# Sparse attention and a two-layer network: the second half of each value tile with its block sums in the first rows, and each half loaded by its own transfer

## The chip, the core and the metric

The kernel runs on one core of one Trainium2 chip. The metric is the device time of one execution in microseconds (us), and a kernel's time is the median over its runs. Each core has five engines with a queue of instructions of its own: TensorE (PE, matmuls; PEld are its weight loads), VectorE (DVE), ScalarE (ACT), GpSimd (POOL) and SyncE (SP). In this kernel SP issues every transfer between the chip's memory (HBM) and the core's working memory (SBUF); matmuls write into a second, smaller memory, PSUM. Engines wait for each other, and for transfers, through semaphores.

## The reference, cut to what matters

There are 4 batches, 8 heads, 768 positions and 64 numbers per head. A query sees the keys less than 16 positions away, and besides them 24 summaries, one for each block of 32 positions. Its key is the block's maximum, its value the block's mean, and its score gets log(32) added. One softmax runs over both, and the result goes through two dense layers with a squared ReLU between them.

```python
k_sum = k.reshape(B, H, nb, block, D).max(axis=3)
v_sum = v.reshape(B, H, nb, block, D).mean(axis=3)
scores_l = scale * np.matmul(q, k.transpose(0, 1, 3, 2))
mask_l = np.abs(pos[:, None] - pos[None, :]) < window
scores_s = scale * np.einsum('bhsd,bhnd->bhsn', q, k_sum) + np.log(block)
a = softmax(concatenate([where(mask_l, scores_l, -1e9), scores_s], axis=-1))
x = np.matmul(a, concatenate([v, v_sum], axis=2))   # then (3072, 512)
h = np.maximum(x @ w_in, 0.0)
out = h * h @ w_out                                  # d_ff = 2048
```

## The kernel before, in words

The 3072 rows are cut into 24 tiles of 128 queries (`g`, six to a batch), and each tile into two halves of 64 queries (`s` = 0 and 1). A half needs 96 keys, its own 64 and 16 on either side, and the 24 block sums of its batch: 120 columns of scores, and 120 rows of values. In the score columns and in the value tile `v_sb`, both halves have the keys in places 0 to 95 and the sums in places 96 to 119.

For each tile and head the kernel does this. `scores` multiplies queries and keys into the `s_ps` banks of PSUM. `mask_max` (DVE) adds the mask and finds the row maximum, `exponentials` (ACT) takes the exponential with the row sum, `inverse` and `norm` (DVE, then POOL) divide by that sum, and `turn` (DVE, 32x32 blocks) or `turn_pe` (PE) transposes the weights into `pT`. `outputs` multiplies them with `v_sb`: 8 matmuls, one a head, for half 0, and then 8 for half 1. `high_x` (ACT) and `low_x` (DVE) split the result into the two parts in which the dense layers take it. `ffn1` and `ffn2` are those layers, for two tiles (256 rows, a chunk) at a time. A float32 matmul shows as two records in the trace, one of the dense layers as one.

The values come by `load_v`, one transfer of 384 KB for both halves of a tile, into rows 0 to 95 of one of two buffers, `v_sb[g % 2]`. A buffer is free again when `outputs` of the tile two before it is done. The value sums are put into rows 96 to 127 of both halves by `place_v0` (batch 0: DVE copies out of PSUM, tokens VC) or `place_v` (later batches: DVE and POOL). The key sums go into chunk 4 of `k_sb` by `place_k` (tokens PK). For the first four tiles `scores_kt` takes keys straight from the transposed keys in `padded` and sums from `ksums`, with two matmuls for each head and half, one for 96 keys and one for 24 sums.

The order of the work on each engine is the order in which the program is written. The start, up to the end of the first two chunks, is a list of tokens (`START`): `L:v1` loads values of tile 1, `S2.0=01` scores of tile 2, `O3=2` the outputs of tile 3, `VC0v` a copy of value sums on DVE (v), ACT (a) or POOL (p), `F1.2.0` and `F2.2.0` steps of the two layers, and `Z6` six matmuls with zeros that fill time. Around the change its order on PE is the scores of tile 4, O1, O0, turning of tiles 2 and 3, the first F1 step, O3, O2, and then the layers almost without a break. On SP it is q4, k4, v1, v0, three weight loads, v3, v2, more weights. After the start, `period` gives each 48 us stretch the same pattern: 8 slots of the dense layers for one chunk, and in their gaps the attention of the next two tiles.

Transfers have eight semaphores (DMAHW0 to 7), taken in turn. So a transfer is not issued before the one eight places ahead of it in SP's queue has landed, and SP holds everything behind it meanwhile.

Of the kernel before, what the change touches and what calls it, by code (L numbers as in the profile page):

```python
# [11 lines left out]
F32 = mybir.dt.float32  # L12
# [58 lines left out]
def attn_ffn_kernel(ctx: ExitStack, tc: tile.TileContext, q, k, kt, v, vt, v0, w, consts, out):  # L73
    nc = tc.nc
    scale = 1.0 / math.sqrt(D)

    const = ctx.enter_context(tc.tile_pool(name="const", bufs=1))
# [9 lines left out]
    mask_sb = consts_sb[:, 0 : 3 * NK].rearrange("q (m c) -> q m c", m=3)  # L87
    id_sb, mean_sb = consts_sb[:, 3 * NK : 3 * NK + P], consts_sb[:, 3 * NK + P :]

    k_sb = [const.tile([P, 5, 2, NPAIR, NB], F32, name=f"k_sb{i}") for i in range(2)]  # L90

    v_sb = [const.tile([P, 2, DM], F32, name=f"v_sb{i}") for i in range(2)]

    q_sb = [const.tile([P, 2, NPAIR, 64], F32, name=f"q_sb{i}") for i in range(2)]
# [3 lines left out]
    ksums = [const.tile([P, NPAIR, NB], F32, name=f"ksum{i}") for i in range(2)]  # L98
# [18 lines left out]
    nc.vector.memset(vsum, 0.0)  # L117
    for t_ in e_bufs + pT:
        nc.gpsimd.memset(t_, 0.0)

    def e_sb(g):
        return e_bufs[g % 2 if g < FROM_PAIRS else 0]

    def copy(eng, out, in_):
        nc.scalar.copy(out=out, in_=in_) if eng is nc.scalar else eng.tensor_copy(out=out, in_=in_)
# [3 lines left out]
        nc.sync.dma_start(out=q_sb[g % 2], in_=q[g // NT, g % NT])  # L129

    def load_k(g):
        nc.sync.dma_start(out=k_sb[g % 2][:, 0:4], in_=k[g - FROM_KT])

    def load_qk(g):
        load_q(g)
        load_k(g)

    def load_v(g):
        nc.sync.dma_start(out=v_sb[g % 2][0:96], in_=v[g // NT, g % NT].rearrange("s j c -> j s c"))

    def sum_v0(vn):

# [10 lines left out]

    def place_v0(ps, j, eng):
        for g in range(2):
            copy(
                eng, v_sb[g][96:128, :, j * P : (j + 1) * P],
                ps[j * 32 : j * 32 + 32, 0:P].unsqueeze(1).to_broadcast([32, 2, P]),
            )

    kv, padded = {}, {}

# [24 lines left out]
        nc.vector.tensor_scalar_mul(vsum[:, p, 0:NB], vsum[:, p, 0:NB], 1.0 / BLOCK)  # L187

    def place_k(g, eng=nc.vector):
        copy(eng, k_sb[g % 2][:, 4], ksums[g // NT % 2].unsqueeze(1).to_broadcast([P, 2, NPAIR, NB]))  # L190

    def place_v(g):
        dst = v_sb[g % 2][96:128]
        if g % 2 == 0:
            for a in range(4):
                nc.vector.transpose(
                    out=dst[:, 0, :].rearrange("a (p c) -> a p c", c=128)[:, :, a * 32 : a * 32 + 32],
                    in_=vsum[a * 32 : a * 32 + 32],
                )
        else:  # L200
            nc.gpsimd.tensor_copy(out=dst[:, 0, :], in_=v_sb[0][96:128, 0, :])
        nc.gpsimd.tensor_copy(out=dst[:, 1, :], in_=v_sb[0][96:128, 0, :])

    w_raw = {}

# [51 lines left out]
    s_ps, nmx, sm = {}, {}, {}  # L257

    def scores(g, p0, p1, banks=None):


        if g not in s_ps:
            at = banks or (g % 2 * 2, g % 2 * 2 + 1)
            s_ps[g] = [bank[n].rearrange("a (p k) -> a p k", p=NPAIR) for n in at]
        for p in range(p0, p1):
            for r, s in ((0, 0), (1, 1), (0, 1), (1, 0)):
                rs, ss = slice(r * 64, r * 64 + 64), slice(s * 64, s * 64 + 64)
                nc.tensor.matmul(  # L268
                    s_ps[g][r][ss, p, 0:NK], lhsT=q_sb[g % 2][rs, s, p, :], rhs=k_sb[g % 2][rs, :, s, p, :],
                    start=True, stop=True,  # L270
                )

    def scores_kt(g, p0, p1, banks=None):

        if g not in s_ps:
            at = banks or (g % 2 * 2, g % 2 * 2 + 1)
            s_ps[g] = [bank[n].rearrange("a (p k) -> a p k", p=NPAIR) for n in at]
        for p in range(p0, p1):
            for k0, k1 in ((0, 96), (96, NK)):
                for r, s in ((0, 0), (1, 1), (0, 1), (1, 0)):  # L280
                    rs, ss = slice(r * 64, r * 64 + 64), slice(s * 64, s * 64 + 64)
                    o = g * P + s * 64
                    keys = ksums[0][rs, p, :] if k0 else padded[p // 2][rs, p % 2, o : o + 96]
                    nc.tensor.matmul(  # L284
                        s_ps[g][r][ss, p, k0:k1], lhsT=q_sb[g % 2][rs, s, p, :], rhs=keys, start=True, stop=True
                    )

    def mask_max(g, h):
# [43 lines left out]

    def turn(g, n0, n1):

        blocks = [(i, j) for i in range(4) for j in ((0, 1, 3) if i % 2 == 0 else (1, 2, 3))]
        for i, j in blocks[n0:n1]:
            nc.vector.transpose(  # L337
                out=pT[g % 2][j * 32 : j * 32 + 32, :, i * 32 : i * 32 + 32],
                in_=e_sb(g)[i * 32 : i * 32 + 32, :, j * 32 : j * 32 + 32],
            )  # L340
# [325 lines left out]
def _masks():  # L666
    m = np.full((3, P, NK), MASKED * math.sqrt(D), np.float32)
    for i, t in enumerate((0, 1, NT - 1)):
        for r in range(P):
            s, u = divmod(r, 64)  # L670
            qp = t * P + s * 64 + u
            for j in range(96):
                kp = t * P - WINDOW + s * 64 + j
                if 0 <= kp < S and abs(qp - kp) < WINDOW:
                    m[i, r, j] = 0.0
        m[i, :, 96:] = np.log(BLOCK) * math.sqrt(D)
    return m


# [7 lines left out]
def _layouts(q, k, v):  # L687
    qd = q.reshape(B, NPAIR, 2, NT, 2, 64, D).transpose(0, 3, 2, 6, 4, 1, 5)
    kp = np.zeros((B, H, S + 2 * WINDOW, D), k.dtype)
    kp[:, :, WINDOW : WINDOW + S] = k  # L690
    vp = np.zeros((B, H, S + 2 * WINDOW, D), v.dtype)
    vp[:, :, WINDOW : WINDOW + S] = v
    kd = np.zeros((B, NT, 2, D, 4, 2, NPAIR, NB), k.dtype)
    vd = np.zeros((B, NT, 2, 96, H, D), v.dtype)
    for s in range(2):
        for t in range(NT):
            o = t * P + s * 64
            kd[:, t, :, :, :, s] = kp[:, :, o : o + 96].reshape(B, NPAIR, 2, 4, NB, D).transpose(0, 2, 5, 3, 1, 4)
            vd[:, t, s] = vp[:, :, o : o + 96].transpose(0, 2, 1, 3)
    return {  # L700
        "q": np.ascontiguousarray(qd).reshape(B, NT, P, 2, NPAIR, 64),
        "k": kd.reshape(B * NT, P, 4, 2, NPAIR, NB)[FROM_KT:],
        "kt": np.ascontiguousarray(k.transpose(0, 1, 3, 2)).reshape(B, NPAIR, P, S),
        "v": vd.reshape(B, NT, 2, 96, DM),
        "vt": np.ascontiguousarray(v.transpose(0, 1, 3, 2)).reshape(B, NPAIR, P, S),
        "v0": np.ascontiguousarray(v[0].reshape(H, NT, P, D).transpose(2, 1, 0, 3)).reshape(P, NT, DM),
    }
# [22 lines left out]
```

## Time and profile before

| | us |
|---|---|
| median of 3 runs | 610.71 (609.70 to 612.49) |
| the profiled execution, its own time | 609.38 |
| its span, first to last instruction | 607.6 |
| PE busy in the span | 595.7 |
| DVE, ACT, POOL busy | 385.6, 265.6, 105.0 |

The profiled execution's time is 1.78 us longer than its span: that is what lies around the program. A row of a timeline begins with the start and the length of a stretch of like instructions, both in us from the span's start; behind it in brackets stands how long the engine had been idle and what ended that. SPq is SP issuing transfers. "DMA to landing" counts from the start of an issue until the data are there, given as least, median and greatest. The granted TensorE clock was 1.00 throughout.

### The profile page before, as it was taken

Reading aid. Unit: us, or ns where it says so; the run is one execution under the profiler, and the core shown is the slowest. Engines: PE = TensorE matmul, PEld = TensorE weight load, DVE = VectorE, ACT = ScalarE, POOL = GpSimd, SP = SyncE. Lnnn points to the kernel's source line nnn. Section 1 sums busy time; section 2 is a strip of 40 time slices with the busy share of each in tenths; the row PEclk is TensorE's granted clock in tenths of the full one; section 3 lists DMA queues with packets and bytes.
Section 4 is the critical chain, followed back from the end, with each engine's and each line's share of the span. In section 5 each row is a group of like instructions: output and inputs, shape, how many; then the busy total and the mean of one; then the engine's idle time right before and its main releaser. Section 6 shows DMA issues by size and latency. Waiting matters only on the chain.

```text
span 607.6 us, 12942 instructions
## 1 busy us (share of the span) xinstructions
PE 595.7 (98%) x5232; PEld 536.8 (88%) x5232; DVE 385.6 (63%) x1063; ACT 265.6 (44%) x687; POOL 105.0 (17%) x97
## 2 busy tenths in 40 slices
PE   8799999999999999999999999999999999999997
PEld 6688899889899989999999989999989989998996
DVE  5889899777647837837545855865663763663121
ACT  4888874343253333433425325425424424422222
POOL 3745765311000101102101101102101010110000
PEclk9999999999999999999999999999999999999999
DMA  8999571350007006006006204202201400200000
GB/s 284 326 352 419 200 260 59 107 185 16 1 22 257 2 2 224 2 2 224 2 2 196 81 2 135 92 1 84 91 2 41 135 1 2 87 1 1 36 0 36
DMA packets 22187, 60.35 MB, mean 99 GB/s; under 512 B 2288, under 2 KB 2288, under 8 KB 20592
## 3 DMA queue, kind: packets, MB, share of 16 engines
q1 hardware_dynamic: 22128, 59.53, 28.6%
q8 instruction: 41, 0.67, 0.4%
q14 instruction: 18, 0.15, 0.1%
HBM read 53.23 MB, written 6.29 MB: 98 GB/s over the span
## 4 chain that ended last, share of the span: by engine, by line
PE 94%; DMA 4%; SPq 0%; ACT 0%; DVE 0%; issue 0%; POOL 0%; POOLq 0%
PE o_ps L425 44%; PE ph L381 39%; PE s_ps L381 4%; PE ph L351 3%; DMA v_sb<-in_v 3%; PE s_ps L268 3%; DMA kv<-in_kt 1%; PE s_ps L284 0%; ACT e_sb L304 0%; SPq L171 0%; PE s_ps L351 0%; POOL e_sb L324 0%; SPq L129 0%; DVE ksum L179 0%; DVE xl L368 0%
## 5 line engine op out<-in xcount | busy, mean ns | idle before, releaser
L381 PE MATMUL ph<-xh,w_sb 128*128 128x256 f32 x1376 | 241.9, 279 | 0.5 <-DVE xl L368 0.5
L425 PE MATMUL o_ps<-w_sb,gh 128*128 128x512 f32 x768 | 238.2, 392 | 0.0
L381 PEld LDWEIGHTS ph<-xh,w_sb 128*128 128x128 f32 x1376 | 213.4, 188 | 8.6 <-issue 1.3
L381 PE MATMUL ph<-xl,w_sb 128*128 128x256 f32 x688 | 190.8, 277 | 0.0
L425 PEld LDWEIGHTS o_ps<-w_sb,gh 128*128 128x128 f32 x768 | 137.2, 188 | 25.0 <-issue 0.3
L425 PE MATMUL o_ps<-w_sb,gl 128*128 128x512 f32 x384 | 151.3, 394 | 0.0
L400 DVE TENSOR_TENSOR ph<-ph,r 128x512 f32<-128x512 f32 x85 | 59.3, 698 | 143.1 <-ACT r L389 142.3
L389 ACT ACTIVATE r<-ph 128x512 f32<-128x512 f32 x84 | 49.9, 594 | 191.0 <-PE ph L381 190.9
L381 PEld LDWEIGHTS ph<-xl,w_sb 128*128 128x128 f32 x688 | 129.5, 188 | 0.0
L337 DVE STREAM_TRANSPOSE pT<-e_sb 32x256 f32<-32x256 f32 x240 | 104.6, 436 | 4.1 <-POOL e_sb L324 0.7
L304 ACT ACTIVATE e_sb<-e_sb,nmx 128x120 f32<-128x120 f32 x192 | 73.6, 385 | 74.3 <-DVE nmx L296 74.3
L324 POOL TENSOR_TENSOR e_sb<-e_sb,total 128x480 f32<-128x480 f32 x47 | 46.2, 991 | 321.7 <-DVE total L318 150.9
L425 PEld LDWEIGHTS o_ps<-w_sb,gl 128*128 128x128 f32 x384 | 72.3, 188 | 14.6
L395 ACT ACTIVATE gh<-r 128x512 fp32r<-128x512 f32 x94 | 59.4, 632 | 13.3 <-PE o_ps L425 6.6
L403 DVE TENSOR_TENSOR gl<-ph,gh 128x512 fp32r<-128x512 f32 x85 | 58.8, 691 | 9.3 <-DVE ph L400 0.5
L296 DVE CUSTOM_DVE_ANT_0 e_sb<-s_ps,consts_sb 128x120 f32<-128x120 f32 x180 | 40.7, 277 | 1.6 <-PE s_ps L284 0.9
L244 POOL TENSOR_TENSOR w_raw<-w_raw 128x1024 int32<-128x1024 int32 (+1 forms) x20 | 35.8, 1792 | 26.0 <-ACT w_raw L235 9.5
L304 ACT ACTIVATION_READ_ACCUMULATOR e_sb<-e_sb,nmx 128x1 f32 x192 | 36.1, 188 | 0.0
L368 DVE TENSOR_TENSOR xl<-ph,xh 128x512 fp32r<-128x512 f32 x22 | 15.2, 690 | 24.4 <-ACT xh L365 24.4
L381 PE MATMUL s_ps<-xh,w_sb 128*128 128x256 f32 x160 | 29.0, 282 | 0.0
L365 ACT CAST xh<-ph 128x512 fp32r<-128x512 f32 x22 | 12.9, 586 | 33.6 <-PE ph L351 33.6
L351 PEld LDWEIGHTS ph<-pT,v_sb 128*64 128x64 f32 x704 | 21.6, 138 | 5.2 <-issue 3.4
(79 smaller groups left out, 412.6 us busy)
## 6 DMA issues: line engine op xcount, KB each, us to landing
w_raw<-in_w SPq DMA_DIRECT2D x12, 1024.0 KB, 13.7
v_sb<-in_v SPq DMA_DIRECT2D x24, 384.0 KB, 4.9
k_sb<-in_k SPq DMA_DIRECT2D x20, 384.0 KB, 6.4
q_sb<-in_q SPq DMA_DIRECT2D x24, 256.0 KB, 5.9
kv<-in_kt SPq DMA_DIRECT2D x16, 384.0 KB, 5.7
out<-ob SPq DMA_DIRECT2D x24, 256.0 KB, 2.0
kv<-in_vt SPq DMA_DIRECT2D x12, 384.0 KB, 6.6
w_raw<-in_w SPq DMA_DIRECT2D x8, 512.0 KB, 7.7
```

Of the source, the lines that this page charges most:

```text
L244: nc.gpsimd.tensor_tensor(out=lo, in0=hi, in1=lo, op=ALU.add)
L296: nc.vector.tensor_tensor_reduce(out=e_sb(g)[:, h, 0:NK], in0=s_ps[g][h % 2][:, h // 2, 0:NK], in1=m, scale=-scale, scalar=3.0e38, op0=ALU ...
L304: nc.scalar.activation(e, e, AF.Exp, bias=nmx[g, half][:, i : i + 1], scale=-1.0, accum_out=sm[g, half][:, i, 0:1])
L324: eng.tensor_mul(out=e, in0=e, in1=sm.pop((g, half)).unsqueeze(2).to_broadcast([P, 4, NK]))
L337: nc.vector.transpose(out=pT[g % 2][j * 32 : j * 32 + 32, :, i * 32 : i * 32 + 32], in_=e_sb(g)[i * 32 : i * 32 + 32, :, j * 32 : j * 32 + ...
L351: nc.tensor.matmul(xp[o : o + 64, h // 2, s * 64 : s * 64 + 64], lhsT=v_sb[g % 2][:, s, h * 64 : h * 64 + 64], rhs=pT[g % 2][:, h, s * 64 ...
L381: nc.tensor.matmul(ph, lhsT=w_sb[f][:, w, cc * P : (cc + 1) * P], rhs=x[c][:, cc, :], start=(n == 0), stop=(n == 3 * NC4 - 1))
L389: nc.scalar.activation(r, ph, AF.Relu)
L395: nc.scalar.activation(gh, r, AF.Square)
L400: nc.vector.tensor_mul(out=ph, in0=ph, in1=r)
L403: nc.vector.tensor_sub(out=gl, in0=ph, in1=gh.bitcast(F32))
L425: nc.tensor.matmul(o_ps[c][tt], lhsT=g_[:, ts_], rhs=w_sb[f][:, w, DM:], start=(first and n == 0), stop=(last and n == 2),)
```

## The change

In the second half (`s` = 1) of every tile the 24 sums now have places 0 to 23, and the 96 keys places 24 to 119, turned by 8: key j stands at place 24 + (j + 8) mod 96. The first half stays as it was. Keys, values and masks are laid out to fit on the host. In the kernel:

- `load_v` issues two transfers of 192 KB, half 0 into rows 0 to 95 and half 1 into rows 24 to 119.
- `place_v0` makes two copies of 128 columns (32 rows for half 0, 24 rows for half 1) in place of one of 2x128; `place_v` writes 24 rows for half 1.
- `k_sb` has ten chunks in place of 5x2: 0 the sums of half 1, 1 to 8 the keys of both, 9 the sums of half 0. `place_k` writes chunks 0 and 9, and `scores` takes every other chunk.
- `scores_kt` needs a third matmul for half 1, since its turned keys are two pieces (88 and 8 columns).
- `turn` transposes other blocks for half 1, as many as before: 12 a tile.
- Two memsets on POOL clear rows 96 to 127 of half 1 at the start, ahead of the memsets of `padded`.

```diff
+TURN = 8
+KEYS_AT = (
+    ((slice(0, 96), 0), (slice(96, NK), None)),
+    ((slice(NB + TURN, NK), 0), (slice(0, NB), None), (slice(NB, NB + TURN), 96 - TURN)),
+)
...
-    k_sb = [const.tile([P, 5, 2, NPAIR, NB], F32, name=f"k_sb{i}") for i in range(2)]
+    k_sb = [const.tile([P, 10, NPAIR, NB], F32, name=f"k_sb{i}") for i in range(2)]
...
+    for t_ in v_sb:
+        nc.gpsimd.memset(t_[96:128, 1], 0.0)
...
     def load_v(g):
-        nc.sync.dma_start(out=v_sb[g % 2][0:96], in_=v[g // NT, g % NT].rearrange("s j c -> j s c"))
+        for s, o in ((0, 0), (1, NB)):
+            nc.sync.dma_start(out=v_sb[g % 2][o : o + 96, s], in_=v[g // NT, g % NT, s])
...
         for g in range(2):
-            copy(
-                eng, v_sb[g][96:128, :, j * P : (j + 1) * P],
-                ps[j * 32 : j * 32 + 32, 0:P].unsqueeze(1).to_broadcast([32, 2, P]),
-            )
+            copy(eng, v_sb[g][96:128, 0, j * P : (j + 1) * P], ps[j * 32 : j * 32 + 32, 0:P])
+            copy(eng, v_sb[g][0:NB, 1, j * P : (j + 1) * P], ps[j * 32 : j * 32 + NB, 0:P])
...
-        copy(eng, k_sb[g % 2][:, 4], ksums[g // NT % 2].unsqueeze(1).to_broadcast([P, 2, NPAIR, NB]))
+        copy(eng, k_sb[g % 2][:, 0:10:9], ksums[g // NT % 2].unsqueeze(1).to_broadcast([P, 2, NPAIR, NB]))
...
-        nc.gpsimd.tensor_copy(out=dst[:, 1, :], in_=v_sb[0][96:128, 0, :])
+        nc.gpsimd.tensor_copy(out=v_sb[g % 2][0:NB, 1, :], in_=v_sb[0][96 : 96 + NB, 0, :])
...
-            for k0, k1 in ((0, 96), (96, NK)):
+            for n in range(3):
                 for r, s in ((0, 0), (1, 1), (0, 1), (1, 0)):
...
+                    if n == 2 and s == 0:
+                        continue
+                    to, first = KEYS_AT[s][n]
...
-        blocks = [(i, j) for i in range(4) for j in ((0, 1, 3) if i % 2 == 0 else (1, 2, 3))]
+        blocks = [(i, j) for i in range(4) for j in ((0, 1, 3), (1, 2, 3), (0, 1, 2), (0, 2, 3))[i]]
```

The order of the instructions shows the change at two places. The first is PE at O3 and O2, the outputs of tiles 3 and 2 in the start; pT_80 and v_sb_74 are the buffers of odd tiles, pT_79 and v_sb_73 those of even ones. Before:

```order
L351 MATMUL s_ps<-pT_80,v_sb_74 64x64 [waits DMAHW5_49,DVE_49]
L351 MATMUL s_ps<-pT_80,v_sb_74 64x64 x3
L351 MATMUL s_ps<-pT_80,v_sb_74 64x64 [waits Activation_49]
L351 MATMUL s_ps<-pT_80,v_sb_74 64x64 x11
L351 MATMUL ph<-pT_79,v_sb_73 64x64 [waits DMAHW6_49]
L351 MATMUL ph<-pT_79,v_sb_73 64x64 x3
L351 MATMUL ph<-pT_79,v_sb_73 64x64 [waits Activation_49]
L351 MATMUL ph<-pT_79,v_sb_73 64x64 x11
```

Now, at the same place on PE:

```order
L361 MATMUL s_ps<-pT_80,v_sb_74 64x64 [waits DMAHW7_49,DVE_49]
L361 MATMUL s_ps<-pT_80,v_sb_74 64x64 x3
L361 MATMUL s_ps<-pT_80,v_sb_74 64x64 [waits Activation_49]
L361 MATMUL s_ps<-pT_80,v_sb_74 64x64 x3
L361 MATMUL s_ps<-pT_80,v_sb_74 64x64 [waits DMAHW0_49]
L361 MATMUL s_ps<-pT_80,v_sb_74 64x64 x7
L361 MATMUL ph<-pT_79,v_sb_73 64x64 [waits DMAHW1_49]
L361 MATMUL ph<-pT_79,v_sb_73 64x64 x3
L361 MATMUL ph<-pT_79,v_sb_73 64x64 [waits Activation_49]
L361 MATMUL ph<-pT_79,v_sb_73 64x64 x3
L361 MATMUL ph<-pT_79,v_sb_73 64x64 [waits DMAHW2_49]
L361 MATMUL ph<-pT_79,v_sb_73 64x64 x7
```

The first eight matmuls of a tile wait for its first transfer, and the ninth waits for its second. The other place is SP's queue in the start, from the load of k4 on (w_raw are weights). Before:

```order
L132 DMA k_sb_71<-in_k 128x768 [waits DMAHW7_49]
L139 DMA v_sb_74<-in_v 96x2x512 [waits DMAHW0_49]
L139 DMA v_sb_73<-in_v 96x2x512
L217 DMA w_raw<-in_w 128x512 [waits DMAHW2_49]
L217 DMA w_raw<-in_w 128x512 [waits DMAHW3_49]
L217 DMA w_raw<-in_w 128x512 [waits DMAHW4_49]
L139 DMA v_sb_74<-in_v 96x2x512 [waits DMAHW5_49,DMAHW0_49,PE_49]
L139 DMA v_sb_73<-in_v 96x2x512 [waits DMAHW6_49,DMAHW1_49,PE_49]
L217 DMA w_raw<-in_w 128x512 [waits DMAHW7_49]
```

Now, on SP from the second transfer of v1 on:

```order
L147 DMA v_sb_74<-in_v 96x512 [waits Pool_49]
L147 DMA v_sb_73<-in_v 96x512 [waits DMAHW2_49]
L147 DMA v_sb_73<-in_v 96x512 [waits DMAHW3_49]
L223 DMA w_raw<-in_w 128x512 [waits DMAHW4_49]
L223 DMA w_raw<-in_w 128x512 [waits DMAHW5_49]
L223 DMA w_raw<-in_w 128x512 [waits DMAHW6_49]
L147 DMA v_sb_74<-in_v 96x512 [waits DMAHW7_49,DMAHW0_49,PE_49]
L147 DMA v_sb_74<-in_v 96x512 [waits DMAHW1_49,PE_49]
L147 DMA v_sb_73<-in_v 96x512 [waits DMAHW2_49,PE_49]
L147 DMA v_sb_73<-in_v 96x512 [waits DMAHW3_49,PE_49]
L223 DMA w_raw<-in_w 128x512
L223 DMA w_raw<-in_w 128x512 [waits DMAHW4_49]
```

The transfers stand in the same order, each of the values in two pieces; the semaphores are handed round faster, so that weight loads wait for other, later transfers than before.

More of the change, by code (lines that the diff above doesn't have):

```diff
@@ L131, in load_k @@
     def load_k(g):
-        nc.sync.dma_start(out=k_sb[g % 2][:, 0:4], in_=k[g - FROM_KT])
+        nc.sync.dma_start(out=k_sb[g % 2][:, 1:9], in_=k[g - FROM_KT])
     def load_qk(g):
@@ L268, in scores @@
                 nc.tensor.matmul(
-                    s_ps[g][r][ss, p, 0:NK], lhsT=q_sb[g % 2][rs, s, p, :], rhs=k_sb[g % 2][rs, :, s, p, :],
+                    s_ps[g][r][ss, p, 0:NK], lhsT=q_sb[g % 2][rs, s, p, :], rhs=k_sb[g % 2][rs, 1 - s :: 2, p, :],
                     start=True, stop=True,
@@ L278, in scores_kt @@
         for p in range(p0, p1):
-            for k0, k1 in ((0, 96), (96, NK)):
+            for n in range(3):
                 for r, s in ((0, 0), (1, 1), (0, 1), (1, 0)):
                     rs, ss = slice(r * 64, r * 64 + 64), slice(s * 64, s * 64 + 64)
-                    o = g * P + s * 64
-                    keys = ksums[0][rs, p, :] if k0 else padded[p // 2][rs, p % 2, o : o + 96]
+                    if n == 2 and s == 0:
+                        continue
+                    to, first = KEYS_AT[s][n]
+                    o = g * P + s * 64 + (first or 0)
+                    width = to.stop - to.start
+                    keys = ksums[0][rs, p, :] if first is None else padded[p // 2][rs, p % 2, o : o + width]
                     nc.tensor.matmul(
-                        s_ps[g][r][ss, p, k0:k1], lhsT=q_sb[g % 2][rs, s, p, :], rhs=keys, start=True, stop=True
+                        s_ps[g][r][ss, p, to], lhsT=q_sb[g % 2][rs, s, p, :], rhs=keys, start=True, stop=True
                     )
@@ L674, in _masks @@
                 if 0 <= kp < S and abs(qp - kp) < WINDOW:
-                    m[i, r, j] = 0.0
-        m[i, :, 96:] = np.log(BLOCK) * math.sqrt(D)
+                    m[i, r, NB + (j + TURN) % 96 if s else j] = 0.0
+            sums = slice(0, NB) if s else slice(96, NK)
+            m[i, r, sums] = np.log(BLOCK) * math.sqrt(D)
     return m
@@ L697, in _layouts @@
             o = t * P + s * 64
-            kd[:, t, :, :, :, s] = kp[:, :, o : o + 96].reshape(B, NPAIR, 2, 4, NB, D).transpose(0, 2, 5, 3, 1, 4)
-            vd[:, t, s] = vp[:, :, o : o + 96].transpose(0, 2, 1, 3)
+            kd[:, t, :, :, :, s] = np.roll(kp[:, :, o : o + 96], s * TURN, axis=2).reshape(B, NPAIR, 2, 4, NB, D).transpose(0, 2, 5, 3, 1, 4)
+            vd[:, t, s] = np.roll(vp[:, :, o : o + 96], s * TURN, axis=2).transpose(0, 2, 1, 3)
     return {
         "q": np.ascontiguousarray(qd).reshape(B, NT, P, 2, NPAIR, 64),
-        "k": kd.reshape(B * NT, P, 4, 2, NPAIR, NB)[FROM_KT:],
+        "k": kd.reshape(B * NT, P, 8, NPAIR, NB)[FROM_KT:],
         "kt": np.ascontiguousarray(k.transpose(0, 1, 3, 2)).reshape(B, NPAIR, P, S),
```

## The prediction

> **What bounds the kernel now.** I read the busy time of the engines in three stretches first: start, middle and end of the span.
>
> ```profile
> core 0: us, PE busy (x) PEld busy (x) DVE busy (x) ACT busy (x) POOL busy (x), PEclk, DMA share, GB/s
> 0.00:37.20 37.20, 29.31 (x553) 24.38 (x553) 27.63 (x123) 24.45 (x85) 20.16 (x27) 1.00 0.96 298
> 37.20:604.10 566.90, 566.40 (x4681) 512.41 (x4680) 357.95 (x941) 240.59 (x601) 84.88 (x70) 1.00 0.25 86
> 604.10:607.60 3.50, 0.00 (x0) 0.00 (x0) 0.00 (x0) 0.58 (x1) 0.00 (x0) 1.00 0.39 150
> ```
>
> From 37.20 on PE is idle for 0.50 of 566.90 us at full clock, while the transfers use a quarter of their time. There the kernel is matmul time, and only PE work can change it. In the first 37.20 us PE is idle for 7.89 us and the transfers are busy 0.96 of the time. So an edit that adds no PE work later acts through one number: when PE gets past O2, the outputs of tile 2, and goes into the unbroken part. The chain of waits in the start, in order of time, says what decides that:
>
> ```profile
> 17.50 10.22 DMA v_sb<-in_v
> ...
> 28.96 7.05 DMA v_sb<-in_v
> 36.01 0.04 issue
> 36.05 1.15 PE ph L351 x32
> ```
>
> The load of v0 from 17.50 to 27.72 (O0 follows, left out here), the load of v2 from 28.96 to 36.01, then O2. The timeline of PE has the idle times ahead of the four outputs, O1, O0, O3 and O2:
>
> ```profile
> 26.38 1.15 PE L351 MATMUL ph<-pT,v_sb 128*64 128x64 f32 x32 [0.78 <-DVE k_sb L125]
> 27.77 1.15 PE L351 MATMUL s_ps<-pT,v_sb 128*64 128x64 f32 x32 [0.23 <-DMA v_sb<-in_v]
> ...
> 33.52 0.28 PE L381 MATMUL s_ps<-xl,w_sb 128*128 128x256 f32 x1
> 34.62 1.15 PE L351 MATMUL s_ps<-pT,v_sb 128*64 128x64 f32 x32 [0.82 <-DMA v_sb<-in_v]
> 36.05 1.15 PE L351 MATMUL ph<-pT,v_sb 128*64 128x64 f32 x32 [0.29 <-DMA v_sb<-in_v]
> 37.14 0.39 PE L381 MATMUL ph<-xh,w_sb 128*128 128x256 f32 x1
> ```
>
> Last, why v2 lands when it does. These are the issues of v1 and v0, of the three weight loads behind them, and of v3 and v2, each with its times to landing:
>
> ```profile
> L139 SPq DMA_DIRECT2D v_sb<-in_v x2: 450/451/452, 17.0 to 17.5; - x2
> DMA to landing us min/median/max: 9.2/9.7/10.2
> L217 SPq DMA_DIRECT2D w_raw<-in_w x3: 454/470/477, 18.0 to 19.0; - x3
> DMA to landing us min/median/max: 10.8/11.7/13.7
> L139 SPq DMA_DIRECT2D v_sb<-in_v x2: 329/329/329, 27.6 to 29.0; - x2
> DMA to landing us min/median/max: 6.9/7.0/7.1
> ```
>
> So v1 lands at 26.2 and v0 at 27.7; the last weights, issued at 19.0, at 32.7; v3, issued at 27.6, at 34.5; v2 at 36.0. Transfers land in the order in which they are issued, after a wait of 7 to 14 us behind the bytes ahead of them. An issue that is a microsecond earlier or later changes no landing.
>
> **The half loads: the gain.** Bytes and order stay. If only bytes count, the second half of v2 lands when the whole lands now, at 36.01, and the first half by half of the 1.5 us between v3 and v2 sooner, about 35.25. O3 does its first half at about 33.8, when the F1 step ahead of it ends, and its second from 34.5, until 35.1. O2 then does half 0 from 35.25, and at 36.05 only half 1 is left: half of the 1.09 us from 36.05 to 37.14, so 0.545. O2 ends at 36.60 in place of 37.14. The term is **-0.54 us**. At O0 the same happens but is hidden, since v2 waits for bytes.
>
> Bounds: if all four waits ahead of outputs vanished, 0.78 + 0.23 + 0.82 + 0.29 = 2.12 us would be gained. If a split transfer costs the queue something of its own, it is a loss; this is the second rival. I take 0.54, since the landings follow the bytes.
>
> **Semaphores and SP.** Of weights and q, four loads now wait for later landings than before. At 33 us all four pieces of v3 and v2 (768 KB) are still outstanding, with weights behind them, so the transfers don't run dry: 0. The issues of the added transfers cost SP 0.33 to 0.45 each (rows above); later on SP spends most of its time waiting for results:
>
> ```profile
> SPq L443 <- ACT ob L125: 425.0, 20, 45.7
> ```
>
> **DVE.** The eight copies of value sums become sixteen of half the length.
>
> ```profile
> 22.62 3.10 DVE L125 COPY v_sb<-o_ps 32x256 f32<-32x256 f32 x8
> ...
> 28.19 0.69 DVE L368 TENSOR_TENSOR xl<-ph,xh 128x512 fp32r<-128x512 f32 x1 [1.05 <-ACT xh L365]
> ```
>
> ```profile
> L125 DVE COPY v_sb<-o_ps 32x256 f32<-32x256 f32 x8 | 3.0, 418 | 0.1
> L125 DVE COPY pT<-s_ps 128x512 f32<-128x512 f32 x2 | 1.4, 688 | 0.0
> ```
>
> From 512 to 256 columns a copy falls by 270 ns, so from 256 to 128 by 135. The eight follow each other at 387 ns, sixteen would at 252: 4.03 us in place of 3.10, **+0.93 us**. Behind them DVE idles for 1.05 us, and O1's matmuls now wait for their own half: its last need is met at about 26.7, it ends near 27.0, where it ends at 27.5 now. Hidden; uncovered, 0.93 less the 0.54. The copies of key sums move the same elements, in two runs in place of one: 0 to a doubling, hidden in the same way.
>
> **PE in the start.** Each of 16 pairs of heads in tiles 0 to 3 gets two matmuls more, four records. The weight loads of tile 2's scores set their pace:
>
> ```profile
> 14.73 0.21 PEld L284 LDWEIGHTS s_ps<-kv,q_sb 64*64 64x64 f32 x8 [0.33 <-DVE nmx L296]
> 14.87 0.23 PEld L284 LDWEIGHTS s_ps<-ksum,q_sb 64*64 64x64 f32 x8
> ```
>
> Eight in 0.14 us, so four in 0.07: 0.28 for a tile, 1.12 us for the four (up to twice that, should the narrow ones overlap less). Of it 0.28, tile 2's, lies ahead of the issue of q4, and tile 0's second two pairs, 0.14, earlier on the same chain. q4, k4, v1 and v0 go out about 0.4 later, into a queue that is full (share 0.96, landings 7 us and more behind their issue), and PE idles before the scores of tile 4:
>
> ```profile
> 24.56 1.05 PE L268 MATMUL s_ps<-k_sb,q_sb 64*64 64x120 f32 x32 [1.64 <-DMA k_sb<-in_k]
> ```
>
> Hidden by this 1.64; uncovered, 1.12.
>
> **POOL.** Two memsets of 512 columns stand ahead of those of `padded`, for which the first scores wait.
>
> ```profile
> L119 POOL MEMSET pT<- 128x1024 f32 x2 | 1.8, 952 | 0.0
> L168 POOL MEMSET kv<- 128x32 f32 x2 | 0.2, 124 | 0.0
> ```
>
> ```profile
> 4.45 0.12 POOL L169 MEMSET kv<- 128x32 f32 x1
> ```
>
> ```profile
> 6.18 0.40 PE L284 MATMUL s_ps<-kv,q_sb 64*64 64x96 f32 x8
> ```
>
> Between 124 and 952 ns, 512 columns lie at 525, two at 1.05: the last memset ends at 5.62 in place of 4.57, before 6.18. Hidden with 0.56 to spare. The later copies of 24 rows in place of 32 keep their 512 columns: 0.
>
> **After the start** PE has the same matmuls, and 20 waits more, each ahead of a ninth matmul. Tiles 12 and 13 have such a wait already (for POOL's copy), tiles 8 and 9 have none. Their outputs:
>
> ```profile
> 213.50 2.08 PE L351 MATMUL ph<-pT,v_sb 128*64 128x64 f32 x64
> 309.38 2.08 PE L351 MATMUL ph<-pT,v_sb 128*64 128x64 f32 x64
> ```
>
> A wait that is met costs nothing that shows. The transfers are busy a quarter of their time there, and no output waits for values. 0.
>
> **The sum** is -0.54 us against the profiled execution: 609.38 to 608.84. The median, 610.71, is 1.33 above that execution; I put the change on the median: 610.71 - 0.54 = **610.2**.
>
> **Rivals.** *The gain is lost downstream.* From 37 to 60 us the weights still arrive by full queues, and PE, 0.54 earlier, might wait for one. The first place to look is F2.0.0, whose second matmul needs DVE's low part of w0:
>
> ```profile
> 42.29 0.73 DVE L253 TENSOR_TENSOR w_sb<-w_raw,w_sb 128x512 fp32r<-128x512 f32 x1
> ```
>
> ```profile
> 44.07 0.62 PE L425 MATMUL o_ps<-w_sb,gh 128*128 128x512 f32 x2
> ```
>
> Ready at 43.02, used from about 44.3: 1.3 us of room, which speaks against it; that other hand-offs have less than 0.54 is possible. Then 610.7.
>
> *A split transfer costs the queue.* This is the way to a slower kernel. 384 KB of values took 1.5 us (34.5 to 36.0). In the stretch behind, the queue moves 420 GB/s:
>
> ```profile
> 37.14:60.00 22.86, 22.86 (x188) 20.89 (x184) 21.38 (x48) 21.01 (x30) 11.31 (x7) 1.00 1.02 420
> ```
>
> At that rate 393,216 bytes take 0.94. If the other 0.56 is a cost of each transfer, four more of them ahead of O2 land its last half 2.24 later, and PE comes out at -0.54 + 2.24 = +1.7: 612.4. It decides from 0.14 us a transfer on. Against it: the rate in the start swings for all loads, and 0.56 may as well belong to rows of 2 KB, which don't change. The Trainium skill, "DMA: Bandwidth & Descriptors", section "Anatomy of one DMA — SWDGE (gpsimd) path", gives a fixed cost of about 2.0 us to each transfer (on GpSimd's path), and its section "Bandwidth" advises transfers of 1 MiB or more; four times 2.0, one behind the other, would make this +7.5. By that rule, v1 and v0 could not land 1.0 to 1.5 us apart, as they do, so most of such a cost overlaps.
>
> *More is gained.* If the smaller pieces let the outputs start without waits, up to 2.12: 608.6. Against it stands the order of landing. That the change does nothing, because PE waits for both halves together, is excluded by the order of its waits.
>
> **How the numbers follow.** The forecast 0.55, lost downstream 0.23, the costly split 0.15, more gained 0.07. 0.5% of 610.71 is 3.05 us, about what a measurement of this kernel can tell from no change. Forecast, lost gain and both bounds lie within it; beyond it are only tails, faster 0.03 (below 607.7, from the last case) and slower 0.06 (above 613.8, from the costly split), so 0.91 for the same. The range takes the forecast with the scatter of the runs (-1.0 and +1.8 about the median) and reaches toward 608.6 and 612.4: 608.8 to 612.3.
>
> **What would show it.** Right: O3 and O2 in two parts of 16 records, the layers behind O2 from about 36.6, then as little idle time on PE as now; sixteen DVE copies at 0.25 each. Wrong: the second half of v2 lands after 36.6, the unbroken part has idle times, or its blocks of outputs take more than 2.08.

## The result, and the profile after

| | before | after |
|---|---|---|
| median of nine runs, us | 609.70 (609.32 to 612.49) | 614.84 (613.09 to 615.59) |
| ratio, 95% interval | | 1.0067 (1.0050 to 1.0084) |
| profiled execution: own time, span | 609.38, 607.6 | 614.93, 612.8 |
| first F1 step behind O2 in the profile | 37.14 | 42.27 |

The forecast was 610.2 with a range up to 612.3; the changed kernel is slower, by 4.1 us after the ratio and by 5.1 between the medians. The busy times by stretch show where. Of the changed kernel, from the start to the end of O2, and from there to the last matmul:

```profile
core 0: us, PE busy (x) PEld busy (x) DVE busy (x) ACT busy (x) POOL busy (x), PEclk, DMA share, GB/s
0.00:42.30 42.30, 33.50 (x617) 28.49 (x617) 28.21 (x129) 24.24 (x85) 21.26 (x29) 0.92 0.76 251
42.30:609.30 567.00, 566.19 (x4682) 511.67 (x4680) 359.61 (x944) 241.09 (x603) 86.17 (x70) 1.00 0.24 87
```

The unbroken part is as long as before (567.00 us, 566.90 then) and PE is idle in it for 0.81 us. All of the loss lies ahead of it: O2 ends 5.1 us later, the granted clock there is 0.92 instead of 1.00, and the transfers, busy for 0.96 of that time before, are busy for 0.76. They no longer set the end. The chain of waits says what does:

```profile
15.98 3.12 PE s_ps L294 x104
19.10 3.04 issue
22.14 0.38 PE s_ps L294 x3
22.52 1.04 PE ph L340 x4
...
26.55 2.45 PE o_ps L156 x48
29.00 0.02 issue
29.03 0.29 DVE v_sb L132
```

Three records before the end of tile 3's scores (L294) PE stands for 3.04 us, and no engine, transfer or semaphore releases it: "issue". Behind the stall the turning (L340) and the value sums (L156) are slow: 1.04 us for four transposes that took 0.60 to 0.66. The clock is the reason. The same kernel in steps of 1 us; the number behind POOL's count is the granted clock:

```profile
core 0: us, PE busy (x) PEld busy (x) DVE busy (x) ACT busy (x) POOL busy (x), PEclk, DMA share, GB/s
20.00:21.00 1.00, 0.00 (x0) 0.00 (x0) 0.00 (x0) 0.42 (x1) 1.00 (x2) 1.00 0.85 300
21.00:22.00 1.00, 0.00 (x0) 0.00 (x0) 0.00 (x0) 0.00 (x0) 1.00 (x2) 0.83 1.02 322
22.00:23.00 1.00, 0.86 (x6) 0.83 (x6) 0.00 (x0) 0.00 (x0) 1.00 (x2) 0.50 0.83 264
...
27.00:28.00 1.00, 1.00 (x28) 0.92 (x24) 0.97 (x10) 1.00 (x6) 0.00 (x0) 0.50 1.03 317
28.00:29.00 1.00, 1.00 (x25) 0.77 (x17) 0.09 (x1) 1.00 (x6) 0.74 (x1) 0.76 0.98 369
```

From the shares of the two end rows the clock is halved from 21.66 (0.83 is 0.66 at 1.00 and 0.34 at 0.50) to 28.48: 6.8 us. The timeline of PE then has the waits of the outputs:

```profile
22.14 0.38 PE L294 MATMUL s_ps<-kv,q_sb 64*64 64x8 f32 x3 [3.04 <-issue]
...
31.19 0.45 PE L361 MATMUL ph<-pT,v_sb 128*64 128x64 f32 x8 [0.84 <-ACT e_sb L314]
33.59 0.92 PE L361 MATMUL ph<-pT,v_sb 128*64 128x64 f32 x24 [1.95 <-DVE v_sb L132]
34.34 1.10 PE L361 MATMUL s_ps<-pT,v_sb 128*64 128x64 f32 x32
...
40.25 1.15 PE L361 MATMUL s_ps<-pT,v_sb 128*64 128x64 f32 x32
41.23 1.10 PE L361 MATMUL ph<-pT,v_sb 128*64 128x64 f32 x32
42.27 0.50 PE L391 MATMUL ph<-xh,w_sb 128*128 128x256 f32 x2
```

O1 waits 1.95 us for DVE's copies of value sums, which the prediction had hidden. O0, O3 and O2 wait for nothing: PE is so late that the values have landed. DVE's copies are the other new row (before: eight in 3.10 us, from 22.62):

```profile
29.03 4.83 DVE L132 COPY v_sb<-o_ps 32x128 f32<-32x128 f32 x16 [0.94 <-PE o_ps L156]
```

So there are two things to explain: a stall that nothing releases, with a slow clock behind it, and copies that take 4.83 instead of 4.03 us. The first theory for the stall: TensorE's instructions are themselves brought by transfers, in blocks, and the next block was not there. The profile has a queue for them:

```profile
q8 instruction: 41, 0.67, 0.5%
```

41 packets carry 0.67 MB, 16 KB each. PE has 5296 matmul records and as many weight loads, 10,592 instructions, so a packet holds about 258 of them, some 129 records. That this queue brings TensorE's instructions and no others rests on this count. Adding up the timeline's counts, PE has done 349 records when it stands. Counted from 0 it stands in front of record 349, and so the records are numbered from here on. The rival: the third matmuls, narrow and on the banks of the other scores, are slow by themselves.

### The profile page after: what moved, and what is told of

Its sections match the earlier page's. It is cut to its first block, busy times and chain, and to the rows that moved or that the text cites. A ratio compares the mean times of both kernels' runs of the same rounds, so it can differ in the third digit from the quotient of the medians.

```text
span 612.8 us, 13130 instructions
## 1 busy us (share of the span) xinstructions
PE 599.7 (98%) x5296; PEld 540.2 (88%) x5296; DVE 387.8 (63%) x1071; ACT 265.9 (43%) x687; POOL 107.4 (18%) x99
## 4 chain that ended last, share of the span: by engine, by line
PE 95%; DVE 2%; issue 1%; DMA 1%; ACT 0%; POOL 0%; SPq 0%; POOLq 0%
PE o_ps L435 43%; PE ph L391 39%; PE s_ps L391 4%; PE ph L361 3%; PE s_ps L274 3%; DMA kv<-in_kt 1%; PE s_ps L294 1%; DVE v_sb L132 1%; PE ph L340 1%; PE o_ps L568 1%; PE o_ps L156 0%; POOL e_sb L334 0%; ACT e_sb L314 0%; PE s_ps L340 0%; DVE w_sb L259 0%
```

## Experiments: each part of the change alone

Three kernels first, one for each suspect (the kernel before, on the same chip, had a median of 609.88). The kernel after without its third matmul (the last 7 or 8 keys of the second halves of tiles 0 to 3 are left out):

```diff
-    ((slice(NB + TURN, NK), 0), (slice(0, NB), None), (slice(NB, NB + TURN), 96 - TURN)),
+    ((slice(NB, NK), -TURN), (slice(0, NB), None)),
...
-            for n in range(3):
+            for n in range(2):
```

> The changed kernel without the third matmul of scores_kt: half 1 of tiles 0 to 3 takes 96 keys in one piece, from 8 places further left, so for these tiles the last 7 or 8 keys of a half are left out and 8 masked-in neighbours stand in their places. PE then has as many matmuls as before the change, and everything else of the change stays. Code theory (PE's instructions come in blocks of 16 KB, and the 64 records that were added make PE use up a block before the next has arrived; it then stands for 3.0 us, and its clock is halved for 6.8 us): no such idle time, clock 1.00, time within 1 us of the kernel before, most likely 0.5 below it. Transfer theory (the split loads cost the queue) and copy theory (sixteen DVE copies hold up O1): 3 to 5 us above the kernel before, as the changed kernel is.

Measured: 611.19, ratio 1.0019 (1.0006 to 1.0032). The stall is gone, F1 starts at 38.47 instead of 42.27. What is left is O1's wait for the copies, and a clock that is halved from 26.3, early in that wait, to 33.1:

```profile
27.42 1.55 PE L359 MATMUL ph<-pT,v_sb 128*64 128x64 f32 x24 [1.29 <-DVE v_sb L132]
28.76 1.92 PE L359 MATMUL s_ps<-pT,v_sb 128*64 128x64 f32 x32
```

Thirty-two records that take 1.10 at full clock take 1.92. The kernel before with the third matmul, and nothing else of the change:

```diff
-            for k0, k1 in ((0, 96), (96, NK)):
+            for n in range(3):
...
+                    if n == 2 and s == 0:
+                        continue
+                    k0, k1 = ((0, 88 if s else 96), (96, NK), (88, 96))[n]
```

> The kernel before, with one thing of the change: half 1's 96 keys in scores_kt in two matmuls of 88 and 8 columns, so 64 records more on PE in the start. Values in one transfer, copies and layout as before. Code theory: PE idle for 2 to 3 us near the end of tile 3's scores, clock halved behind it, 3 to 5 us above the kernel before. Narrow-matmul theory (a matmul of 8 columns is itself what stops PE): the same. Transfer and copy theories: no more than 1 us above.

Measured: 612.89, ratio 1.0055 (1.0037 to 1.0072), F1 at 40.61. The stall is there, again ahead of record 349:

```profile
22.39 0.38 PE L287 MATMUL s_ps<-kv,q_sb 64*64 64x8 f32 x3 [2.15 <-issue]
```

So the third matmul carries most of the loss. The kernel before with half loads alone:

```diff
-        nc.sync.dma_start(out=v_sb[g % 2][0:96], in_=v[g // NT, g % NT].rearrange("s j c -> j s c"))
+        for s in range(2):
+            nc.sync.dma_start(out=v_sb[g % 2][0:96, s], in_=v[g // NT, g % NT, s])
```

> The kernel before, with one thing of the change: each value tile loaded by two transfers, both into rows 0 to 95. Transfer theory: 2 to 5 us above the kernel before. Code theory: no idle time of PE at tile 3's scores, 0.5 us below the kernel before, as forecast for the half loads alone, or level with it.

Measured: 609.40, ratio 0.9985 (0.9965 to 1.0005). Its chain of waits:

```profile
28.42 7.28 DMA v_sb<-in_v
35.70 0.04 issue
35.74 0.69 PE ph L352 x16
36.43 2.94 PE ph L382 x24
```

O2's second half waits for the second transfer until 35.70, and the 16 records of that half are all that stands behind it. In the timeline F1 starts at 36.36 instead of 37.14. Neither a cost of the split nor a loss downstream shows. Run again with more rounds:

> The kernel before with the values of each tile loaded by two transfers, as in the earlier run of this edit (ratio 0.9985, 0.9965 to 1.0005), with more rounds: whether 0.7 us earlier at the first F1 step behind O2 is a real gain. If it is: ratio 0.998 to 0.9995 with an interval that ends below 1. If the gain is lost downstream: ratio 0.9995 to 1.0005.

Measured: 609.32, ratio 0.9990 (0.9972 to 1.0007), with F1 at 37.04 in its profile. The sign agrees both times, and both intervals take in 1: whether a gain of some 0.7 us survives can't be told from these runs.

## Experiments: is it the number of instructions?

First the kernel before with 60 records of zeros at the very start, in place of five of the fillers there (the tokens of `START`, and in `zeros` ahead of its loop):

```diff
-Z15 XT L:q0 L:kv0
+Z10 XT L:q0 L:kv0
...
+            for i in range(30):
+                rs = slice(i % 2 * 64, i % 2 * 64 + 64)
+                nc.tensor.matmul(
+                    z_ps[0][rs, 0:24], lhsT=zero32[rs].to_broadcast([64, 64]),
+                    rhs=zero32[rs].to_broadcast([64, 24]), start=True, stop=True,
+                )
```

> The kernel before, with nothing of the change. 30 small matmuls of zeros (60 records of 24 columns) stand at the very start in place of 5 of the 15 large ones, while PE only fills time before the first keys have landed. The scores themselves keep their matmuls. Code theory: every block boundary now lies 60 records earlier in the work, PE is idle for about 2 us near the end of tile 3's scores, perhaps with a halved clock behind it, and the time is 1.5 to 4.5 us above the kernel before. Narrow-matmul, transfer and copy theories: within 0.5 us of the kernel before.

Measured: 611.21, ratio 1.0017 (1.0003 to 1.0031), less than expected. The small matmuls left PE at half its pace (a filler took 0.46 us, at full clock 0.23) and delayed the first scores by 2.6 us. Record 349 now lies in the turning of tile 1, behind the scores of tile 3. There the timeline of PE shows 1.38 us of waiting and names POOL, but what POOL wrote was there at 21.1, and the weight load that needed it ran. The weight loads (PEld) show who stood:

```profile
21.14 0.14 PEld L330 LDWEIGHTS ph<-consts_sb,e_sb 128*128 128x128 f32 x1 [0.20 <-POOL e_sb L324]
22.73 0.35 PEld L330 LDWEIGHTS ph<-consts_sb,e_sb 128*128 128x128 f32 x3 [1.45 <-issue]
```

The matmul of the first, record 349, came at 22.73 too, and nothing but its own place in the stream held it. So the stall is there, with 1.4 us. A second one came one block later, in O0, ahead of record 476:

```profile
30.67 1.76 PE L351 MATMUL s_ps<-pT,v_sb 128*64 128x64 f32 x27 [0.83 <-issue]
```

476 is 349 and 127, about the records of one packet. A cleaner test puts 64 such records where PE waited for 1.21 us anyway, ahead of T0.0. The kernel before, with a token Y that issues such matmuls of 24 columns with zeros:

```diff
-S1.1=45 Z5 E0.0
+S1.1=45 Z5 Y32 E0.0
...
+        elif op == "Y":
+            for n in range(i):
...
```

> The kernel before, with 32 zero matmuls of 24 columns (64 records of TensorE) added where TensorE waits 1.21 us ahead of T0.0; scores, copies and loads as before. Code theory (a block of instructions of TensorE ends at its record 349 and the next one is not there before about 22): record 349 now lies in the scores of tile 3, at about 18.1 to 18.7 us, in place of the end of the value sums at 22.4; there TensorE stands without a releaser for 2 to 3.5 us, the granted clock falls to 0.5 behind it, and the time is 611.5 to 613.5. Rival (the stall belongs to the third matmuls, narrow matmuls on the same banks as the scores): no such stall, clock 1.00, 609.5 to 610.5.

Measured: 611.90, ratio 1.0031 (1.0019 to 1.0044), F1 at 40.59:

```profile
18.77 0.38 PE L284 MATMUL s_ps<-kv,q_sb 64*64 64x96 f32 x8
18.97 0.25 PE L284 MATMUL s_ps<-ksum,q_sb 64*64 64x24 f32 x5
22.20 0.41 PE L284 MATMUL s_ps<-ksum,q_sb 64*64 64x24 f32 x3 [2.98 <-issue]
22.53 1.11 PE L330 MATMUL ph<-consts_sb,e_sb 128*128 128x128 f32 x4
```

Five of eight matmuls of one kind run, then PE stands for 2.98 us ahead of record 349, and the clock halves behind it. Nothing in the scores was changed. The rival falls: what counts is the number of instructions ahead, not what they are. (The profiled execution, 613.20, was the slowest of five; the others took 611.40 to 612.24.)

Can PE be kept busy meanwhile? The changed kernel with twelve matmuls with zeros ahead of the last half of tile 3's scores:

```diff
-S3.1=30 AD1.1 S3.0=30
+S3.1=30 AD1.1 Z12 S3.0=30
```

> The changed kernel, with twelve matmuls with zeros (2.7 us) ahead of the last quarter of tile 3's scores, so that TensorE works while it stood for 3.04 us. Code theory: what is left of the stall is under 0.8 us, since the instructions arrive at the same time; no idle window, so the granted clock stays 1.00, T, Z and the value sums take half as long as in the changed kernel, and the first F1 step behind O2 comes at about 38.5 to 39.5 in place of 42.27: 611 to 612 us. Rival (TensorE stands at the third matmuls for a reason of their own): the 3.0 us come after the zeros as before, the first F1 step at 44 or later, 616 or more. Second rival (the clock is not what costs, but only the stall): the clock is 1.00 and F1 still comes at 41.5 or later.

Measured: 615.76, ratio 1.0099 (1.0081 to 1.0117), F1 at 43.73: a miss, on four runs from 614.70 to 617.26. The stall moved behind the zeros and was still 2.58 us:

```profile
18.26 2.89 PE L568 MATMUL o_ps<-zero 128*128 128x512 f32 x12
...
24.41 0.30 PE L294 MATMUL s_ps<-kv,q_sb 64*64 64x88 f32 x2 [2.58 <-issue]
```

That spoke for another version of the theory: the block is asked for only when PE comes to its end. Twice as many zeros tell:

```diff
-S3.1=30 AD1.1 S3.0=30
+S3.1=30 AD1.1 Z24 S3.0=30
```

> The changed kernel with 24 matmuls with zeros (5.4 us) instead of twelve ahead of the last quarter of tile 3's scores, so that TensorE comes to its record 349 at about 24.5. Theory i (the load of the next block is asked for when TensorE enters a block, at record 221, about 16.4, and takes 5.3 to 8.0 us, as in the runs so far): it is there by 24.4, the stall is under 0.5 us, no issue wait of note. Theory ii (the block is asked for only when TensorE comes to its end; the stall of 2 to 3 us behind twelve zeros spoke for it): the stall is again 2 to 3 us, at 24.5 to 27.5. The time by i: about 616 to 617 (5.4 us of zeros less the stall of 3.0 and the time of the halved clock); by ii 618 to 620.

Measured: 616.80, ratio 1.0114 (1.0073 to 1.0155), F1 at 43.10, on two runs only. No issue stall is left:

```profile
17.78 5.51 PE L568 MATMUL o_ps<-zero 128*128 128x512 f32 x24
23.22 0.40 PE L294 MATMUL s_ps<-kv,q_sb 64*64 64x96 f32 x8
23.43 0.27 PE L294 MATMUL s_ps<-ksum,q_sb 64*64 64x24 f32 x8
```

The block is asked for early, then: its packet passes at 19.5, and PE comes to record 349 only at 23.5. The transfers in steps of 0.1 us show when its packet passes. Of the changed kernel, from 19.70 to 19.80:

```profile
q8 instruction: 1, 0.02, 63.2%
```

With twelve zeros, from 21.90 to 22.00:

```profile
q8 instruction: 1, 0.02, 59.1%
```

With the third matmul alone the packet is at 20.0, with the tiny matmuls at 19.8. PE goes on at 22.14, 24.41, 22.39 and 22.20: each time 2.3 to 2.5 us behind it. With the sixty records at the very start the packets are at 20.3 and 28.2, and PE goes on at 22.73 and 30.67, 2.4 behind either. And PE enters the block ahead, at its record 221 if that begins 128 records earlier, at about 16.4 in the changed kernel, so the packet comes 3.3 us after that; in the run with twelve zeros it came 5.6 after it. Was that chance, or did the zeros do it? With twice the zeros in the same place it came 3.6 after, which speaks for chance. The same twelve in two places:

```diff
-S3.1=30 AD1.1 S3.0=30
+Z6 S3.1=30 AD1.1 Z6 S3.0=30
```

> The changed kernel with the same twelve matmuls with zeros in two places, six ahead of the first and six ahead of the second half of tile 3's scores. In five of the six runs whose packets were looked at, the instruction packet comes 3.3 to 3.6 us after TensorE enters the block ahead, in the run with twelve zeros in one place 5.5, and TensorE goes on 2.4 us after the packet in all four that stall. If that one packet was late by chance of the transfer queue: packet at about 19.8, TensorE goes on at about 22.2, the stall is under 0.8 us and no half clock follows it; the first F1 step behind O2 at about 41.5, 613 to 614 us. If the zeros themselves make it late: packet near 22, a stall of 2 to 3 us, 615.5 or more.

Measured: 614.80, ratio 1.0078 (1.0049 to 1.0107). The packet passes at 19.6, and at 22.0 PE runs again; of the stall some 0.4 us are left, in the middle of this row's eleven records:

```profile
21.53 0.76 PE L294 MATMUL s_ps<-kv,q_sb 64*64 64x8 f32 x11
...
25.08 1.52 PE L156 MATMUL o_ps<-vn,consts_sb 128*32 128x128 f32 x48
```

The clock stays 1.00 until 31.2, the value sums take 1.52 us again instead of 2.47, and F1 starts at 41.48, as expected for a packet that was late by chance. The median, 614.80, is above the expected 613 to 614, though: with PE at full clock but 22 us gone at record 349, what stood behind it in the changed kernel still stands there. O1 waits 0.89 and 1.95 us as before, and that wait now halves the clock from 31.2 on.

## Experiments: the copies

The kernel before with sixteen copies in place of eight, all into rows 96 to 127:

```diff
-            copy(
-                eng, v_sb[g][96:128, :, j * P : (j + 1) * P],
-                ps[j * 32 : j * 32 + 32, 0:P].unsqueeze(1).to_broadcast([32, 2, P]),
-            )
+            for s in range(2):
+                copy(eng, v_sb[g][96:128, s, j * P : (j + 1) * P], ps[j * 32 : j * 32 + 32, 0:P])
```

> The kernel before, with the value sums placed by sixteen copies of 32x128 in place of eight of 32x256; nothing else. Copies theory: sixteen copies take 4.0 to 4.8 us in place of 3.10, end 0.9 to 1.7 later, O1 waits for them instead of having its last need met at once, and the time is 0.7 to 1.5 above the kernel before (610.5 to 611.5), more if the clock is halved as in the variant with two matmuls. Rival (what is left with two matmuls comes from elsewhere, the placement of sums or the loads): the copies are hidden by DVE's 1.05 us of idle time, 609.6 to 610.2.

Measured: 609.82, ratio 0.9999 (0.9989 to 1.0009): hidden, as the prediction had it, and the copies theory in this form falls. But look at the timeline of DVE:

```profile
23.39 3.64 DVE L125 COPY v_sb<-o_ps 32x128 f32<-32x128 f32 x16
```

Sixteen copies take 3.64 us here and 4.83 in the changed kernel, 0.23 against 0.30 each. There they alternate between rows 96 to 127 and rows 0 to 23. The next kernel is the one with two matmuls, with its copies in another order:

```diff
         for g in range(2):
             copy(eng, v_sb[g][96:128, 0, j * P : (j + 1) * P], ps[j * 32 : j * 32 + 32, 0:P])
+        for g in range(2):
             copy(eng, v_sb[g][0:NB, 1, j * P : (j + 1) * P], ps[j * 32 : j * 32 + NB, 0:P])
```

> The variant with two matmuls (it leaves out the last keys of the second half in tiles 0 to 3), with the four copies of a token in another order: both of half 0, rows 96 to 127, first, then both of half 1, rows 0 to 23. Hold theory (a DVE copy whose output starts in another group of 32 rows than the one ahead of it waits until that is finished: 0.302 us for one in place of 0.203, from 16h = 4.83 with two matmuls and 4h + 12u = 3.64 with sixteen copies in the kernel before): eight held, eight not, 4.0 us for the sixteen; O1's wait for DVE falls from 1.3 to about 0.5, the granted clock stays 1.00, and the time is 610.0 to 610.6 against 611.2 with two matmuls. Rival (copies of 24 rows, or into rows 0 to 23, are slow by themselves): 4.8 us as before, wait, clock and time as with two matmuls.

The groups by shape, with busy time and mean of one, for the kernel with two matmuls:

```profile
L132 DVE COPY v_sb<-o_ps 32x128 f32<-32x128 f32 x8 | 2.3, 290 | 0.1
L132 DVE COPY v_sb<-o_ps 24x128 f32<-24x128 f32 x8 | 2.3, 285 | 0.1
```

and with the copies grouped:

```profile
L132 DVE COPY v_sb<-o_ps 32x128 f32<-32x128 f32 x8 | 2.0, 284 | 0.2 <-PE o_ps L156 0.2
L132 DVE COPY v_sb<-o_ps 24x128 f32<-24x128 f32 x8 | 2.0, 279 | 0.1
```

One copy is as long as before (284 and 290 ns); the sum falls from 4.6 to 4.0, since they overlap. O1 waits for no copy any more, F1 starts at 36.79 instead of 38.47, and the time is 609.84, ratio 0.9984 (0.9962 to 1.0006) against 1.0019. The clock was still halved, for 3.4 us from 26.3, which the expectation had not; ahead of it PE had waited 1.81 us for k4. Copy by copy the trace shows what is held, here and with sixteen copies in the kernel before: a copy into the same rows as the one ahead starts 0.20 to 0.22 us after it; one into other rows, or the first of a token, which reads other rows of PSUM, starts 0.28 to 0.31 after it. By the Trainium skill, "VectorE: DVE Perf Modes", section "Two Vector instructions with no wait between them", an instruction whose output starts in another group of 32 partitions than the last one's is held until every earlier one has finished; the trace agrees, at about 0.1 us for each (0.302 held and 0.203 not, as expected beforehand).

Last, the change with both faults taken out. Keys of half 1 in their natural order need no third matmul, at the price of a thirteenth block to transpose on DVE, and the copies are grouped:

```diff
-TURN = 8
+TURN = 0
...
-    ((slice(NB + TURN, NK), 0), (slice(0, NB), None), (slice(NB, NB + TURN), 96 - TURN)),
+    ((slice(NB, NK), 0), (slice(0, NB), None)),
...
-        blocks = [(i, j) for i in range(4) for j in ((0, 1, 3), (1, 2, 3), (0, 1, 2), (0, 2, 3))[i]]
+        blocks = [(i, j) for i in range(4) for j in ((0, 1, 3), (1, 2, 3), (0, 1, 2), (0, 1, 2, 3))[i]]
```

> The changed kernel with the keys of half 1 in places 24 to 119 in their natural order (no turn by 8), so that two matmuls do for each head and half in tiles 0 to 3, with thirteen blocks in place of twelve to transpose on DVE for each later tile, and with the copies grouped by rows; everything is computed. If instruction blocks and held copies are all that the change cost: no issue stall at record 349, copies 4.0 us, clock 1.00, the first F1 step behind O2 at 37.0 to 37.8, time 609.5 to 610.5 (the thirteenth block is hidden on DVE, which is busy for two thirds of the time). If something else of the change costs (the two memsets on POOL, the wait ahead of the ninth output matmul): 611 or more with neither stall nor halved clock.

Measured: 609.25, ratio 0.9994 (0.9975 to 1.0014). The loss is gone. No stall is at record 349. In its profiled execution q of tile 3 landed late (a wait of 1.8 us, and O1 waits 0.8 for the copies, with a clock of 0.50 behind either), so that F1 came at 39.16, later than the 37.0 to 37.8 expected; nine other runs hold the median.

## Why the prediction was wrong, point by point

**PE in the start: this step failed.** It costed the 64 added records by their time, 1.12 us, and named the 1.64 us ahead of tile 4's scores as cover. The size was fair, but a record is also a place in TensorE's stream of instructions. In the kernel before, record 349 lies at the end of the value sums:

```profile
20.98 1.52 PE L148 MATMUL o_ps<-vn,consts_sb 128*32 128x128 f32 x48
```

PE came there at 22.2; the packet had passed at 19.2, so the block was ready at about 21.6, with some 0.6 us to spare (0.1 in the first profile of the half loads). Of this margin the profile of before shows nothing, since nothing waited. With the added records 349 lies in tile 3's scores, where small matmuls follow each other at some 20 ns, and PE is there at 19.10. Much of what it had done by 22.2 in the kernel before (most of the turning of tiles 0 and 1, the value sums) still lay ahead, at half clock. Alone this costs 3.4 us (0.0055 of 609.9). That the place is set by the number of instructions is shown (the same stall with zeros in an unchanged program, at 349 and one packet further at 476, none when PE comes late enough). That PE waits for that very packet was not measured by itself; it rests on the 2.3 to 2.5 us between the two in all seven cases, and in no profile does PE pass record 349 sooner behind the packet. What sets the 2.9 to 5.6 us from entering a block to its packet was varied by no edit. The traces speak for the full transfer queue: at the next boundary, record 476, the packet came 0.3 to 1.1 us behind PE in the six profiles in which the transfers were all but idle just then (busy share 0.00 to 0.09), and 1.6 to 6.2 us in the other eight (0.92 to 1.04).

The Trainium skill has the mechanism, on "Runtime: NRT & Kernel Launch", section "Instruction fetch mechanics": blocks of 16 KB, 256 instructions, of which the next is fetched while the current one runs. The trace agrees in size (258 a packet). The section holds the cost of crossing into a new block for mostly hidden, since instructions are issued more slowly than blocks arrive; here 3.04 us were not, and the measurement decides.

**The clock** was 1.00 in the profile of before and no term of the sum. In every profile its stretches, but for the last, are whole multiples of 3.41 us (in the changed kernel 17.07 at 1.00, then 6.83 at 0.50), so windows of that length can be laid off from its changes. Each halved stretch in the start follows a window in which PE idled for 1.65 us or more, 2.56 in the changed kernel. Windows with up to 1.64 us, as around the wait for k4 in the kernel before, left the clock at 1.00, and so did one with 1.69; the ends of matmuls are modelled, so the limit can only be put near half a window. The 2.58 us in the run with twelve zeros halved nothing because they fell into two windows, 1.23 and 1.35. A halved stretch lasted one window where PE idled in it for 0.40 us or less, and two where it idled for 0.48 or more. "TensorE: Matmul & The Clock Gate", Part 1 of the Trainium skill, gives free-running windows of 3413 ns, of which an idle one halves the clock; the length agrees. But in no window was PE idle throughout, 2.80 us at most, so the rule here is milder than "idle".

**DVE: the size was off.** Sixteen copies were put at 4.03 us by their columns. The step from 256 to 128 columns was right (418 to about 285 ns for one copy); the spacing was not. The eight copies of before follow each other at 0.34 to 0.35 and 0.42 to 0.44 us in turn, the longer step where a token begins, and their mean hid that. In rows 96 to 127 alone sixteen take 3.64 and are hidden as forecast; alternating between two groups of rows they take 4.83, and the cover named, 1.05 us, doesn't reach: O1 waits 1.29 us, largely within a stretch at half clock, and the time is 611.19. Grouped they take 4.0, and O1 waits for none of them.

**The half loads: the mechanism right, the size not settled.** -0.54 was forecast; in the two profiles of that edit alone F1 comes 0.78 and 0.10 earlier, and the times are 0.9 and 0.6 us lower, with intervals that take in no gain at all. The costly split would have been 2.2 us on the other side and falls. The loss downstream stays possible at this size. More gain, from outputs that wait for nothing, is not there: the chain still waits for the last transfer. In the changed kernel itself the gain has no place, because PE comes after the values.

**Memsets, semaphores, the rest: right.** POOL's two memsets took 0.99 us for 1.05 forecast and delayed nothing. In the unbroken part the 20 added waits don't show; the outputs of tiles 8 and 9 take what they took:

```profile
218.52 2.08 PE L361 MATMUL ph<-pT,v_sb 128*64 128x64 f32 x64
```

The parts add up roughly: 3.4 for the third matmul alone and 1.2 for all else of the change together (two matmuls; copies and half loads are in it) make 4.6, where the ratio gives 4.1 and the medians 5.1. In part the two are the same wait: with the third matmul alone O1 already waits 1.08 us for the eight old copies, since the value sums come late, and 1.95 in the changed kernel.

## What to carry to other kernels

Instructions added in a stretch of short ones have a price apart from their time: count the records to the next block boundary, and see whether the engine gets there sooner than before and how long its block takes to come. An "issue" wait in the middle of like instructions is the sign of it (once it stood under the name of another engine that had long been done, and only the weight loads showed it), and the instruction queue's packets give its time. And when idle time on TensorE is used as cover, add up what is left idle in 3.4 us: here, from about half of that on, the clock was halved, and a second wait can cost more than itself.

## What the hardware showed that was not expected

- TensorE stood for 2.15 to 3.04 us ahead of its matmul record 349 in four kernels, and for 1.4 us there and 0.83 us ahead of record 476 in a fifth, with nothing to wait for but its instructions; it goes on 2.3 to 2.5 us behind a packet of the instruction queue.
- A window of 3.41 us with 1.65 us or more of idle time on TensorE is followed by half the clock, one with up to 1.64 is not (one with 1.69 was not either); waits of 1.64 and 0.78 us fell into two windows in the kernel before and halved nothing, 1.55 and a part of 1.29 shared one in the run with two matmuls and did.
- DVE copies of 128 columns cost 0.30 us each where their rows alternate between two groups of 32, and 0.23 on average where they don't, though one copy alone is as long.
- Sixty records of small matmuls did not bring TensorE to full pace at the start: the fillers behind them ran at 0.46 us each, twice the 0.23 at full clock (the profile's own clock column reads 1.00 there, so this goes by the pace). From the run with the zeros at the very start:

```profile
0.92 3.40 PE L559 MATMUL o_ps<-zero 64*64 64x24 f32 x60 [0.92 <-DVE zero L114]
4.25 4.63 PE L564 MATMUL o_ps<-zero 128*128 128x512 f32 x10
```
